# A recurrent attention kernel: two streamed weights put into PSUM by VectorE as 32-bit words, copied back by two engines, and queries turned ahead of the first half's normalization

## The chip, the core and the metric

The kernel runs on one core of a Trainium2 chip. The metric is the device time of one execution in microseconds. TensorE, VectorE, ScalarE, GpSimd and SyncE each work through their own queue of instructions in order and wait for one another by semaphores; the DMA engines move data beside them. In the profile's tables PE is TensorE, PEld its weight loads, DVE VectorE, ACT ScalarE, POOL GpSimd and SP SyncE.

## The reference

The output is the sum of the input, of an attention that carries a memory from segment to segment, and of a dense layer. Both branches read the input after a layer norm without scale and shift.

```python
xn = _layernorm(x)                                  # x: 1 x 2048 x 1024, bf16
# branch A: 64 segments of 32 rows, one after the other, M = 8 memory rows
for s in range(64):
    h = concat([mem, xn[:, 32*s:32*s+32]])          # 40 rows
    q, k, v = h @ Wq, h @ Wk, h @ Wv                # 1024 -> 32 heads x 128
    p = softmax(where(mask, q @ k.T / sqrt(128), -1e9))
    o = (p @ v) @ Wo                                # 40 x 1024
    mem = o[:, :8]                                  # memory of the next segment
    outs.append(o[:, 8:])
# branch B
gelu(xn @ w1 + b1, approximate=True) @ w2 + b2      # 1024 -> 3584 -> 1024
return x + concat(outs) + B
```

The mask has a row for each query and a column for each key: memory queries see every key, the others the keys up to their own place, `(idx[:, None] < M) | (idx[:, None] >= idx[None, :])`. Each segment needs the memory that the segment before it made, so the segments can't run side by side.

## The kernel before, in words

**First part, up to about 419 us.** Layer norm and the dense branch: four groups of 512 rows, with w1 and w2 in SBUF. In its last group the places that w1, w2 and their intermediate results leave are filled with attention weights.

**Second part.** The 64 segments. The weights Wq, Wk, Wv and Wo, 32 MB together, are cut into 64 units of 512 KB (128 partitions x 2048 bf16). A segment uses every unit once, in a fixed order: eight K units of the first half of the heads ("half 0"), eight Q units of half 0, K and Q of half 1, V of both halves, then sixteen units of Wo (the O phase). 46 units stay in SBUF. 18 are "streamed": they come again in every segment through a ring of six slots (tile name `u`). When TensorE has used a streamed unit, `unit_done` calls `start_stream`, which fills the freed slot with the next streamed unit, by a DMA from a copy in DRAM (`Wc_K`, `Wc_Q`, `Wc_V`, `Wc_O`) on SyncE's queue.

Two of the 18 come from PSUM and not from DRAM: `IN_PSUM`, the Q unit 4 of half 0, and `IN_BANKS`, the O unit 14. They lie in four PSUM banks (`kept`), put there in segment 0 by `keep`. In later segments `start_stream` copies them back into a slot (L247), two copies of 128 x 1024 bf16 each: those of IN_PSUM begin when the first K unit of the segment is done, those of IN_BANKS when O unit 7 is done ("in the K phase" and "in the O phase" below). `keep` in the kernel before goes through TensorE: it transposes 128 x 128 blocks into the bank `mixed`, copies them to SBUF on VectorE and ScalarE, and transposes them back into `kept`. The second unit's two halves wait for it in `d_oL` and `half_home`.

**Main rows and left rows.** A segment multiplies its 8 memory rows and 24 of its 32 new rows as "main rows" (`hT`); the last 8 new rows of four segments ("left rows", `hL`) are multiplied together once in four segments, each weight in a segment of its own. With i4 the segment's number modulo 4: Q of half 0 in i4 = 1, Q of half 1 in i4 = 2, K of half 0 in i4 = 3, K of half 1 in i4 = 0, V of half 0 in i4 = 0, V of half 1 in i4 = 3, Wo in i4 = 1. Segment 0 does all K, Q and V. The turned left queries are kept in `qL`; where the next group's will overwrite queries that are still needed, `keep_q` first saves these in spare columns of the bank `mixed` (`qS`), and `q_left` takes them from `qL` or, at i4 = 2 and 3 for half 0 and at i4 = 3 for half 1, from `qS`.

**Inside a segment.** `half_pass` issues the products of one half of one weight into a PSUM accumulator (`acc`, three banks, handed out by `new_acc` and `let_go`) and calls the functions in `at` after the named units. `turn_k` and `turn_q` copy an accumulator to SBUF (ScalarE, L758) and transpose it in blocks of 32 (VectorE, L772); `turn_kL` and `turn_qL` do the same for left rows with VectorE alone. `scores` multiplies queries and keys into `mixed` (L816, L822), takes the exponential (ScalarE, L828) and applies the mask (VectorE, L833). `sums` adds the exponentials by matmul into `mixed` (L841, L847), takes Ln and twice Exp on ScalarE (L852, L855), and multiplies with the result on VectorE (L862, L866); `values` multiplies by V (L881, L887) and copies out (L895). The scores of half 0 are computed after the first Q unit of half 1, their sums after its last; those of half 1 after V units 0 and 4 of half 1. At the end, `put_mem` (L282, L286) puts the new memory rows into `hT`.

The order on each engine is that of the program: the schedule is written out by hand. A framework adds the semaphore waits from what instructions read and write. So where a function is called decides what stands behind what.

Of the kernel before, what the change touches and what calls it, by code (L numbers as in the profile page):

```python
# [10 lines left out]
BF16 = mybir.dt.bfloat16  # L11
# [6 lines left out]
P = 128  # L18
# [68 lines left out]
def kernel(  # L87
# [151 lines left out]

    def start_stream(slot):  # L240
        if not starts:
            return
        n = starts.popleft()
        unit, t = streams[n], slab(slot)
        if unit in kept_in:
            for c0, bank in kept_in[unit]:
                nc.vector.tensor_copy(out=t[:, c0:c0 + 1024], in_=bank)  # L247
# [45 lines left out]
    with tc.tile_pool(name="ma", bufs=2) as ma, tc.tile_pool(name="mps", bufs=6, space=PSUM) as mps:  # L293
# [191 lines left out]
        for tg in range(4):  # L485
# [81 lines left out]
            else:  # L567
# [7 lines left out]
                put_mem(o_sb, nxt["hT"], mps.tile([P, 512], F32, name="ps"))  # L575
                pss = [mps.tile([P, 512], F32, name="ps") for _ in range(6)]
# [28 lines left out]
                nc.sync.dma_start(out=d_oL[:, :], in_=Wo_v[:, h + 1, :])  # L605
# [6 lines left out]
    with tc.tile_pool(name="late", bufs=1) as late, \  # L612
# [28 lines left out]
        kept = banks.tile([P, 4, 1024], BF16, name="kept")  # L641

        def copy_bits(out, in_):

            nc.vector.tensor_single_scalar(out=out, in_=in_, scalar=0, op=ALU.bitwise_or)

        def keep(unit, c0, w, bank):

            turned = [late.tile([P, 512], BF16, name=f"VL{n}").rearrange("p (k t) -> p k t", k=4) for n in range(2)]
            for n in range(2):  # L650
                for k in range(4):
                    nc.tensor.transpose(trs[n][:, k, :], w[:, 512 * n + P * k:512 * n + P * (k + 1)], ident)
                (nc.scalar.copy if n else nc.vector.tensor_copy)(out=turned[n], in_=trs[n])
            for n in range(2):
                for k in range(4):
                    c1 = 512 * n + P * k
                    nc.tensor.transpose(kept[:, bank, c1:c1 + P], turned[n][:, k, :], ident)
            kept_in.setdefault(unit, []).append((c0, kept[:, bank, :]))
# [31 lines left out]
        for s in range(NSEG):  # L690
# [145 lines left out]
            def sums(u):  # L836
# [17 lines left out]
                for b in (1, 0):  # L854
# [3 lines left out]
                    )  # L858
                pdA = pd_main.rearrange("p (c b q) -> p c b q", c=4, b=2)
# [56 lines left out]

            psK, psKL = half_pass("K", 0, left_k[0], {})
# [3 lines left out]
            psQ, psQL = half_pass("Q", 0, left_q[0], {})  # L921
            if first:
                keep(IN_BANKS, 1024, d_oL, 2)
                keep(IN_BANKS, 0, half_home, 3)
                nc.sync.dma_start(out=part_home, in_=Wo_v[:, 4 * PART[1] + 2 * PART[2], 0:PART_COLS])
                copy_bits(mixed[:, 468:512].bitcast(U32), mask.bitcast(U32))
                for t in outs:
                    nc.vector.memset(t[:, :, 0:32], 0.0)
# [31 lines left out]
            at = {0: [lambda: scores(1)], 4: [lambda: sums(1)]}  # L960
# [132 lines left out]
```

## Time and profile before

| | |
|---|---|
| time, median of three | 1892.51 us (1891.93 to 1899.58) |
| span of the profiled execution | 1887.0 us |
| segment 0 of the attention | 419 to 467.6 us |
| one later segment, mean | 22.4 us |
| PE, busy | 1729.5 us (92%) |
| DVE, busy | 921.3 us (49%) |
| ACT, busy | 637.6 us (34%) |
| DVE copies from `kept` (L247) | 254, 163.3 us, 685 ns each |
| DMA, mean | 328 GB/s |

A segment's start is taken as the start of L286 in VectorE's timeline, which ends the segment before. Busy time of TensorE is not work at its peak, since matmuls overlap. A wait's row names who waited, for whom, the total, how many times and the longest, in us. A timeline's row has start, duration, engine, line, operation, tiles and shapes, and in brackets the idle time just before and what ended it; a row can stand for several instructions in a run.

### The profile page before, as it was taken

To read this page: it belongs to the slowest core of one execution; us is meant where nothing else is said; L and a number is where in the kernel's file an instruction comes from. 1 tells how busy PE (TensorE), PEld (TensorE's weight loads), DVE (VectorE), ACT (ScalarE), POOL (GpSimd) and SP (SyncE) were. 2 spreads that over 40 slices of the span, in tenths; PEclk is the share of its full clock that TensorE was granted. 3 is DMA by queue.
4 is the path that set the end of the run, shared out by engine and by line. 5 is a ranking of instruction groups with operands and counts; after the bars stand their busy time and mean duration, and the time that the engine had idled before them with its cause. 6 is when DMAs were issued, how large, how long until landed. Compare 5 with 4: busy or idle time off the path is not lost.

```text
span 1887.0 us, 72995 instructions
## 1 busy us (share of the span) xinstructions
PE 1729.5 (92%) x32255; PEld 940.0 (50%) x32275; DVE 921.3 (49%) x2222; ACT 637.6 (34%) x1356; POOL 277.2 (15%) x538
## 2 busy tenths in 40 slices
PE   7999999997998989999999999899999999988987
PEld 3444444444454545455555555455545454555544
DVE  6657474603454444444454445444444454444443
ACT  6334352502333333333333333333333333333332
POOL 0000000000341111111121111212121111111112
PEclk9999999998999999999999999999999999999999
DMA  9821211498999999999999999999999999999998
GB/s 337 269 52 45 55 47 50 172 351 278 401 395 377 372 377 356 378 391 395 391 392 383 387 369 390 370 386 387 385 398 386 392 398 380 387 380 369 376 379 325
DMA packets 220025, 618.39 MB, mean 328 GB/s; under 512 B 47243, under 2 KB 65595, under 8 KB 219708
## 3 DMA queue, kind: packets, MB, share of 16 engines
q1 hardware_dynamic: 199292, 593.57, 83.0%
q0 software_dynamic: 16320, 17.52, 2.8%
q8 instruction: 252, 4.13, 0.9%
q10 hardware_dynamic: 4096, 2.64, 0.5%
q14 instruction: 65, 0.53, 0.1%
HBM read 599.39 MB, written 30.34 MB: 334 GB/s over the span
## 4 chain that ended last, share of the span: by engine, by line
PE 67%; DMA 19%; DVE 7%; ACT 3%; issue 3%; POOL 0%; ACTq 0%; DVEq 0%; POOLq 0%; SPq 0%
PE acc L714 32%; PE ps L503 10%; PE acc L907 10%; DMA u<-Wc_K 9%; PE ps L552 8%; DMA u<-Wc_O 5%; DMA u<-Wc_Q 3%; PE ps L587 2%; ACT mixed L855 2%; PE acc L881 2%; DVE b_oL L772 1%; DMA outL_d<-half_home 1%; DVE pd_main L862 1%; PE mixed L816 1%; DVE u L247 1%
## 5 line engine op out<-in xcount | busy, mean ns | idle before, releaser
L714 PE MATMUL acc<-u,hr_home 128*32 128x512 bf16 x11520 | 781.5, 382 | 32.4 <-DMA u<-Wc_K 13.6
L714 PEld LDWEIGHTS <-hr_home 128*32 128x32 bf16 x12288 | 350.8, 97 | 321.5 <-issue 72.1
L714 PE MATMUL acc<-u,hrL 128*32 128x512 bf16 x2880 | 256.3, 381 | 12.4 <-issue 6.1
L503 PE MATMUL ps<-u 128*128 128x512 bf16 x896 | 194.9, 380 | 2.6 <-ACT u L387 2.6
L907 PE MATMUL acc<-u,d_oL 128*32 128x256 bf16 (+1 forms) x3552 | 177.2, 292 | 12.3 <-DMA u<-Wc_O 7.9
L247 DVE COPY u<-kept 128x1024 bf16<-128x1024 bf16 x254 | 163.3, 685 | 25.7 <-PE acc L907 9.1
L552 PE MATMUL ps<-u 128*128 128x512 bf16 x657 | 146.2, 379 | 0.8
L907 PEld LDWEIGHTS <-b_oL 128*32 128x32 bf16 (+1 forms) x3552 | 109.1, 98 | 75.0 <-issue 40.9
L503 PEld LDWEIGHTS <-u 128*128 128x128 bf16 x896 | 87.9, 98 | 108.4 <-issue 3.1
L907 PEld LDWEIGHTS <-d_oL 128*32 128x32 bf16 (+1 forms) x3552 | 104.4, 99 | 63.8 <-issue 20.7
L862 DVE TENSOR_TENSOR pd_main<-half_home,mixed 128x320 bf16<-128x320 bf16 x128 | 62.5, 488 | 150.1 <-ACT mixed L855 147.6
L907 PE MATMUL acc<-u,b_oL 128*32 128x256 bf16 (+1 forms) x1665 | 108.7, 290 | 19.3 <-DVE u L247 8.8
L714 PEld LDWEIGHTS <-hrL 128*32 128x32 bf16 x3072 | 90.4, 96 | 66.3 <-issue 24.7
L772 DVE STREAM_TRANSPOSE b_oL<-b_oL 128x512 bf16<-128x512 bf16 x128 | 90.6, 708 | 66.8 <-ACT b_oL L758 66.8
L907 PE MATMUL acc<-W_O,b_oL 128*32 128x256 bf16 (+1 forms) x1776 | 108.3, 289 | 4.9 <-issue 4.6
L758 ACT CAST kT<-acc 128x512 bf16<-128x512 f32 x64 | 37.5, 586 | 219.7 <-PE acc L714 219.7
L259 POOL DMA_DIRECT2D hr_home<-hr_d x58 | 32.7, 564 | 528.7 <-PE acc L714 528.7
L552 PEld LDWEIGHTS <-u 128*128 128x128 bf16 x672 | 65.3, 98 | 77.4 <-DVE g_u L519 0.4
L758 ACT CAST b_oL<-acc 128x512 bf16<-128x512 f32 x128 | 75.2, 588 | 80.5 <-PE acc L714 80.5
L833 DVE TENSOR_TENSOR half_home<-half_home,mixed 128x96 bf16<-128x96 bf16 (+1 forms) x256 | 37.6, 188 | 127.4 <-ACT half_home L828 127.3
L1002 ACT CAST d_oL<-acc 128x256 bf16<-128x256 f32 (+1 forms) x63 | 26.9, 427 | 214.2 <-PE acc L907 214.2
L855 ACT ACTIVATE mixed<-mixed,small_consts 128x160 f32<-128x160 f32 x256 | 94.3, 368 | 8.4
(129 smaller groups left out, 2033.3 us busy)
## 6 DMA issues: line engine op xcount, KB each, us to landing
u<-Wc_K SPq DMA_DIRECT2D x320, 512.0 KB
u<-Wc_V SPq DMA_DIRECT2D x256, 512.0 KB
u<-Wc_O SPq DMA_DIRECT2D x256, 512.0 KB
u<-Wc_Q SPq DMA_DIRECT2D x128, 512.0 KB
u<-Wc_O SPq DMA_DIRECT2D x64, 384.0 KB
u<-in_B_w_dram SPq DMA_DIRECT2D x14, 512.0 KB
u<-in_A_Wq_dram SPq DMA_DIRECT2D x14, 512.0 KB
u<-in_A_Wv_dram SPq DMA_DIRECT2D x12, 512.0 KB
```

Of the source, the lines that this page charges most:

```text
L247: nc.vector.tensor_copy(out=t[:, c0:c0 + 1024], in_=bank)
L503: nc.tensor.matmul(ps[:, :].rearrange("p (s t) -> p s t", t=SEG), lhsT=w1_sb[fb // 14 * 8 + kt][:, (fb % 14) * P:(fb % 14 + 1) * P], rhs=x ...
L552: nc.tensor.matmul(ps[:, :], lhsT=gts[fc // 4][:, fc % 4, t * P:(t + 1) * P], rhs=w2_sb[fc // 2][:, fc % 2, cs], start=(fc == 0), stop=(fc ...
L587: nc.tensor.matmul(pss[2 * t + nb][:, :], lhsT=gts[fc // 4][:, fc % 4, t * P:(t + 1) * P], rhs=w2_sb[fc // 2][:, fc % 2, nb * 512:nb * 512 ...
L714: nc.tensor.matmul(o, lhsT=lhs[:, i, :], rhs=m, start=(i == seq[0]), stop=(i == seq[-1]), tile_position=(0, 32 * j),)
L758: cp(out=out, in_=ps.rearrange("p (h e) -> p h e", e=32))
L772: nc.vector.transpose(out=home, in_=home)
L833: nc.vector.tensor_tensor(out=p, in0=p, in1=m[:, None, :].to_broadcast([P, 4, n]), op=ALU.min)
L855: nc.scalar.activation(out=mixed[:, 160 * b:160 * b + 160], in_=mixed[:, 0:160], func=ACT.Exp, scale=-1.0, bias=off[:, b:b + 1],)
L862: nc.vector.tensor_tensor(out=pdA.rearrange("p c b q -> p b c q"), in0=prA[:, None, :, :].to_broadcast([P, 2, 4, 40]), in1=dd, op=ALU.mult,)
L881: nc.tensor.matmul(oV[r][:, c, :, :], lhsT=V[q, c * P:(c + 1) * P], rhs=pdA[q, c, :, :], start=(c == 0), stop=False, skip_group_check=True ...
L907: nc.tensor.matmul(acc[r:r + n // 8, 0:n], lhsT=lhs[:, 4 * (i % 4) + 2 * u + k, :], rhs=w_t[:, c0:c0 + n], start=(unit == O_UNITS[0] and k ...
```

## The change

The parts:

1. `keep` writes `kept` by one VectorE instruction for each half unit, a bitwise or with 0 on 32-bit words (`copy_bits`), straight from SBUF. The two halves of IN_BANKS are put away before the first K pass of segment 0 (they were put away after its first Q pass), and the DMA that brings `d_oL` is issued before the last dense products.
2. `start_stream` copies the first 1024 columns back by `copy_bits` on VectorE and the others by a ScalarE copy.
3. In later segments `q_left` is called after unit 2 of the Q pass and `keep_q` after unit 3; they were called after the pass.
4. The two products on VectorE at the end of `sums` become `normalize`. For half 0 it is called after `turn_q` of half 1, so that VectorE turns the queries first; for half 1 its place is as before.

They are to take the put-away off TensorE's queue, relieve VectorE of half the copies, and let VectorE turn queries while ScalarE computes the reciprocal of the sums.

```diff
+    def copy_bits(out, in_):
+        nc.vector.tensor_single_scalar(out=out, in_=in_, scalar=0, op=ALU.bitwise_or)
...
             for c0, bank in kept_in[unit]:
-                nc.vector.tensor_copy(out=t[:, c0:c0 + 1024], in_=bank)
+                if c0:
+                    nc.scalar.copy(out=t[:, c0:c0 + 1024], in_=bank.bitcast(BF16))
+                else:
+                    copy_bits(t[:, c0:c0 + 1024].bitcast(U32), bank.bitcast(U32))
...
                 put_mem(o_sb, nxt["hT"], mps.tile([P, 512], F32, name="ps"))
+                nc.sync.dma_start(out=d_oL[:, :], in_=Wo_v[:, h + 1, :])
...
                 fetch_resident("xt2", "xt3")
-                nc.sync.dma_start(out=d_oL[:, :], in_=Wo_v[:, h + 1, :])
...
         def keep(unit, c0, w, bank):
-            turned = [late.tile([P, 512], BF16, name=f"VL{n}").rearrange("p (k t) -> p k t", k=4) for n in range(2)]
-            for n in range(2):
-                for k in range(4):
-                    nc.tensor.transpose(trs[n][:, k, :], w[:, 512 * n + P * k:512 * n + P * (k + 1)], ident)
-                (nc.scalar.copy if n else nc.vector.tensor_copy)(out=turned[n], in_=trs[n])
-            for n in range(2):
-                for k in range(4):
-                    c1 = 512 * n + P * k
-                    nc.tensor.transpose(kept[:, bank, c1:c1 + P], turned[n][:, k, :], ident)
+            copy_bits(kept[:, bank, :].bitcast(U32), w.bitcast(U32))
             kept_in.setdefault(unit, []).append((c0, kept[:, bank, :]))
...
+            def normalize(u):
+                prA, prB = st["pr", u]
                 pdA = pd_main.rearrange("p (c b q) -> p c b q", c=4, b=2)
...
+            if first:
+                keep(IN_BANKS, 1024, d_oL, 2)
+                keep(IN_BANKS, 0, half_home[:, :], 3)
+                nc.sync.dma_start(out=part_home, in_=Wo_v[:, 4 * PART[1] + 2 * PART[2], 0:PART_COLS])
+                copy_bits(mixed[:, 468:512].bitcast(U32), mask.bitcast(U32))
+                for t in outs:
+                    nc.vector.memset(t[:, :, 0:32], 0.0)
             psK, psKL = half_pass("K", 0, left_k[0], {})
...
-            psQ, psQL = half_pass("Q", 0, left_q[0], {})
+            at = {} if first else {2: [lambda: q_left(0)]}
+            if left_q[0] and not first:
+                at[3] = [lambda: keep_q(0)]
+            psQ, psQL = half_pass("Q", 0, left_q[0], at)
             if first:
-                keep(IN_BANKS, 1024, d_oL, 2)
-                keep(IN_BANKS, 0, half_home, 3)
...
                 turn_qL(psQL, 0)
-            q_left(0)
+                q_left(0)
             turn_q(psQ)
             if left_q[0] and not first:
-                keep_q(0)
                 turn_qL(psQL, 0)
...
+            if not first:
+                at[2] = [lambda: q_left(1)]
+                if left_q[1]:
+                    at[3] = [lambda: keep_q(1)]
             psQ1, psQ1L = half_pass("Q", 1, left_q[1], at)
             if first:
                 turn_qL(psQ1L, 1)
-            q_left(1)
+                q_left(1)
             turn_q(psQ1)
+            normalize(0)
             if left_q[1] and not first:
-                keep_q(1)
                 turn_qL(psQ1L, 1)
...
-            at = {0: [lambda: scores(1)], 4: [lambda: sums(1)]}
+            at = {0: [lambda: scores(1)], 4: [lambda: sums(1), lambda: normalize(1)]}
```

More of the change, by code (lines that the diff above doesn't have):

```diff
@@ L640 @@
         mask_left = masks_at[:, NX:].rearrange("p (g q) -> p g q", g=GRP)
[L641 to L645 removed]
+        kept = banks.tile([P, 4, 512], F32, name="kept")
         def keep(unit, c0, w, bank):
[L649 to L657 removed]
+            copy_bits(kept[:, bank, :].bitcast(U32), w.bitcast(U32))
             kept_in.setdefault(unit, []).append((c0, kept[:, bank, :]))
@@ L920 @@
                 turn_kL(psKL, 0)
-            psQ, psQL = half_pass("Q", 0, left_q[0], {})
+            at = {} if first else {2: [lambda: q_left(0)]}
+            if left_q[0] and not first:
+                at[3] = [lambda: keep_q(0)]
+            psQ, psQL = half_pass("Q", 0, left_q[0], at)
             if first:
-                keep(IN_BANKS, 1024, d_oL, 2)
-                keep(IN_BANKS, 0, half_home, 3)
[L925 to L928, printed above, removed]
                 turn_qL(psQL, 0)
-            q_left(0)
+                q_left(0)
             turn_q(psQ)
             if left_q[0] and not first:
-                keep_q(0)
                 turn_qL(psQL, 0)
```

## The prediction

> **What bounds the kernel now.** I read the page's slices first, then the windows, the waits, and last the timelines of the first segment and of one later segment.
>
> The windows: stretch, busy time by engine, granted clock, DMA share, GB/s.
>
> ```profile
> 420.00:470.00 50.00, 39.94 (x747) 21.92 (x740) 17.84 (x39) 10.92 (x23) 1.82 (x4) 0.90 0.81 279
> 480.00:580.00 100.00, 90.75 (x2024) 53.26 (x2020) 45.81 (x109) 32.27 (x75) 37.52 (x68) 1.00 1.02 396
> 1500.00:1600.00 100.00, 92.44 (x2142) 51.99 (x2133) 48.96 (x115) 33.21 (x78) 16.25 (x30) 1.00 1.00 387
> ```
>
> The reader is to see two regimes. From segment 1 on, the DMA engines have a share of 1.00 and TensorE some 90%: both are full, and neither has much to give. The first segment (419 to 467.6 us) is another place: TensorE at 80% of its time, DMA at 0.81 and 279 GB/s. Only there does something other than these two set the pace.
>
> What it is, on TensorE in the first segment (start, duration, instructions, idle time before):
>
> ```profile
> 427.16 0.40 PE L657 MATMUL kept<-pd_main,VL 128*128 128x128 bf16 x4 [0.46 <-ACT VL L653]
> ...
> 429.42 0.40 PE L657 MATMUL kept<-pd_main,VL 128*128 128x128 bf16 x4 [0.46 <-ACT VL L653]
> 429.75 0.40 PE L714 MATMUL acc<-u,hr_home 128*32 128x512 bf16 x4
> ...
> 432.82 0.40 PE L652 MATMUL mixed<-pd_main,d_oL 128*128 128x128 bf16 x4 [1.59 <-DMA d_oL<-in_A_Wo_dram]
> ```
>
> The transposes of `keep` and their copies hold TensorE from 425.2 to 429.75 and, with the wait for `d_oL`, from 431.2 to 438.3.
>
> The waits (who waited for what: total, times, longest), in all segments together:
>
> ```profile
> DVE pd_main L862 <- ACT mixed L855: 147.6, 111, 3.5
> ...
> PE mixed L816 <- DVE b_oL L772: 19.5, 30, 1.0
> ...
> PE acc L907 <- DMA u<-Wc_O: 16.6, 45, 0.9
> PE acc L714 <- DMA u<-Wc_K: 13.6, 26, 1.2
> ...
> PE mixed L816 <- DVE mixed L645: 9.1, 14, 0.7
> ...
> PE acc L907 <- DVE u L247: 8.8, 14, 0.7
> ```
>
> VectorE's large wait for the exponentials costs only what is queued behind it: the turned queries, for which TensorE waits 19.5 us. `keep_q` costs 9.1 us, the copies back 8.8 us. Together 37 us in 63 segments, against 30 us of waits for streamed weights.
>
> One segment of those whose number leaves 3 by 4 ("type 3"), on VectorE:
>
> ```profile
> 1060.32 0.70 DVE L939 STREAM_TRANSPOSE d_oL<-d_oL 128x512 bf16<-128x512 bf16 x1
> 1060.95 0.65 DVE L758 CAST kL<-acc 128x512 bf16<-128x512 f32 x1
> 1061.64 0.71 DVE L772 STREAM_TRANSPOSE kL<-kL 128x512 bf16<-128x512 bf16 x1
> 1062.40 0.49 DVE L862 TENSOR_TENSOR pd_main<-half_home,mixed 128x320 bf16<-128x320 bf16 x1
> 1062.81 0.28 DVE L866 TENSOR_TENSOR pd_left<-half_home,mixed 128x128 bf16<-128x128 bf16 x1
> 1063.01 0.22 DVE L794 COPY b_oL<-mixed 128x128 bf16<-128x128 bf16 x1
> 1063.14 0.70 DVE L772 STREAM_TRANSPOSE b_oL<-b_oL 128x512 bf16<-128x512 bf16 x1
> ```
>
> TensorE starts the sums of this half at 1060.90, long before VectorE reaches the query copy of L794.
>
> **What the Trainium skill says.** "VectorE: DVE Perf Modes", section "Walkthrough: the 8-slice pipeline in each mode": two packed 16-bit elements go through per cycle, a 32-bit element from PSUM one. So the word copy of 512 is no slower than the copy of 1024 halves; the trace agrees (681 ns for 128x1024 bf16 in L247, 685 for a cast of 128x512 f32). "ScalarE: Activation LUTs", section "What ACT_TABLE_LOAD costs": 186 ns and 0.833 ns an element, bf16 or not; the trace has 586 ns for 512, a little under it. "DMA: Bandwidth & Descriptors", section "Specifications": 435 GB/s is the ceiling of the fabric; the windows reach 396, so the stream has little more in it.
>
> **The change part by part.**
>
> *Start.* `keep` as four word copies, about 0.67 us each on VectorE, beside the K and Q passes; VectorE has 4.2 us of idle time there. TensorE loses the two stretches, 4.6 + 7.1 = 11.6 us. The wait of 2.3 us for the left queries' bank, at 450.4, where VectorE first waited for the exponentials, goes also; slow matmuls (granted clock 0.90, about 3 us) may go. New: `d_oL` came at about 432.8 behind the last resident weights, and the next streamed units are issued right after it, from 428.9, as before. TensorE then arrives some 2 us before its first Q unit of half 1. The cap is the stream: (390 - 279) GB/s over these 50 us is 14 us of transfer time, of which some is blocked ahead of 428.9. I take 12 us saved, ends 8 and 15.
>
> *Copies back.* The two halves of one slot, now on two engines, look parallel. In the built order of the changed kernel they are not: in the O phase VectorE's copy waits for ScalarE's of the same slot, in the K phase ScalarE's for VectorE's. A pair took 1.29 us; now 0.67 + 1.02 (586 + 512 x 0.84, the slope between the 320 and the 512 element casts, 426 and 586 ns; the page gives 1.04) + 0.06 to cross = 1.75. In the K phase 0.46 us more lies within the margin before the Q unit (0.5 us at the least, 1.3 mostly). In the O phase TensorE needs the slot 6 units x 0.216 = 1.3 us after the copies can start. Type 3: VectorE was held by two casts until 0.88 and done at 2.16; ScalarE now begins at 0.1, so VectorE is done at 1.83: 0.3 us better. Type 0: done at 1.38, now 1.83, of which some 0.2 us shows. Types 1 and 2 arrive later than that (512-wide products, waits for Wc_O): nothing.
>
> *Queries ahead of normalization.* The cast of the queries still stands behind the exponentials on ScalarE and ends 0.51 us after them; the transpose can start there instead of at 0.74. Scores begin 0.2 us sooner in types 1 and 3. But the two products of L862 and L866 (0.69 us) now come after the transpose, and values need them: first at 2.0 us after the exponentials, against 2.06 in type 1 and 2.30 in type 3. In type 2 values need a bank that the left queries' cast frees behind those products: 2.70 against 2.44, 0.26 us worse, while the 0.33 us won at the scores is spent waiting there.
>
> *`q_left` and `keep_q` inside the pass.* This adds a wait. They touch the bank `mixed`; the sums' matmuls write it; being earlier in the program, they are now waited for by the sums. Type 3: the query copy stands behind the cast and transpose of kL: L939's end 1061.02 + 0.58 + 0.75 + 0.25 = 1062.6, where the sums started at 1060.90: 1.7 us, with the whole V pass queued behind on TensorE. Type 2: keep_q ends about 0.36 us after L939's end; the sums began 0.15 us before that end on average: 0.5 us. Type 1 and 0: no such wait.
>
> *Sum for TensorE's chain in four segments:* type 3 1.7 - 0.2 - 0.3 = 1.2; type 2 0.5 + 0.26 = 0.76; type 0 0.2; type 1 -0.06: together about 2.0 us, in 15 groups 31 us. Not all shows: TensorE waits for weights 1.1 us in type 2 and 0.6 in type 1, and where it arrives later it waits less. On the other hand the stream is fed by the slots TensorE frees. By the gaps of unexplained origin in this trace (0 to 2.7 us a segment, 43 in all), a microsecond lost on TensorE lengthened its own segment by 0.9, and that and the next together by 0.65, with wide scatter. I take 0.4, about 12 us, with ends 0 and 0.9 (28 us).
>
> **Rivals.** *Given back (forecast):* 1892.5 - 12 + 12 = 1892. *The saturated stream absorbs the new waits:* the shares of 1.00 speak for it, the waits for DMA of only half a microsecond a segment against; 1892.5 - 12 + 2 = 1882, faster. *The new waits are paid in full and more than eat the start:* the gaps' effect speaks for it, the waits for weights against; 1892.5 - 12 + 28 = 1908, slower. *Nothing of the wait on `mixed` is real and 37 us of waits fall by half:* 1892.5 - 12 - 18 = 1862; the order of the built program speaks against it.
>
> **How the numbers follow.** Forecast 0.48, absorbed 0.25, paid in full 0.24, the last 0.03. The bound of 0.5% is 9.5 us. Faster 0.28, same 0.46, slower 0.26; a part of the forecast's case lies outside the bound on no preferred side. The range is from 1879 (start at 14, nothing lost) to 1908.
>
> **What would show it.** After: no matmuls into `kept`; segment 0 ends at about 454 instead of 467.6 (right start); the sums waiting for the query copy 1.7 us in type 3 and for `keep_q` 0.5 us in type 2 (a row of about 30 us in all); the wait of scores for turned queries down by a fifth to a third; copies back of 1.0 us on ScalarE, end to end with VectorE's. Wrong if segments of types 2 and 3 are no longer than before, if segment 0 still ends after 460, or if ScalarE's copies delay the casts behind them so that K or Q passes wait.

## The result, and the profile after

The changed kernel took 1905.76 us (median of four runs, 1903.54 to 1906.91) against 1892.22 us (four runs, 1891.34 to 1899.58) of the kernel before: a ratio of 1.0062, 95% interval 1.0035 to 1.0089. It is slower by some 12 us, clear of the noise. That is near the end of the predicted range (1908) and not at the predicted 1892.

The windows of the changed kernel, with the columns of those shown of before (stretch, busy time by engine, granted clock, DMA share, GB/s):

```profile
420.00:470.00 50.00, 41.52 (x867) 22.93 (x869) 24.30 (x51) 15.54 (x31) 6.93 (x13) 1.00 0.94 345
480.00:580.00 100.00, 91.33 (x2100) 50.75 (x2100) 41.11 (x101) 40.57 (x81) 37.28 (x68) 1.00 1.02 393
1500.00:1600.00 100.00, 87.61 (x2058) 49.52 (x2052) 41.37 (x103) 41.56 (x87) 17.10 (x33) 1.00 0.99 372
```

The first stretch is better: 345 GB/s instead of 279 (over segment 0 alone 350 instead of 268). The last is worse: TensorE's busy time falls from 92.4 to 87.6 us in 100, and the stream from 387 to 372 GB/s, while the DMA share still reads 0.99. By VectorE's timeline segment 0 now takes 36.9 us (423.4 to 460.3) instead of 48.6, and the 62 after it, up to the last new memory, 1415.8 us instead of 1392.0. So the change won 11.7 us once and lost 23.7 us over the rest. (A part of this is the clock. From 366 to 424 us the granted clock was 1.00 before and 0.94 after, and the dense part ended 4.4 us later; from 420 to 470 us it was 0.90 before and 1.00 after, so that not all of the 11.7 us is the change's doing.)

Where the 23.7 us are, in the waits of the changed kernel (who for what: total, times, longest):

```profile
PE mixed L811 <- DVE pd_left L863: 46.3, 47, 1.1
...
PE mixed L836 <- DVE b_oL L789: 19.6, 15, 1.4
PE acc L709 <- DMA u<-Wc_K: 17.4, 30, 2.0
...
PE acc L904 <- DMA u<-Wc_O: 11.1, 32, 0.9
...
PE mixed L836 <- DVE mixed L242: 6.9, 10, 1.2
```

Three rows are new, and they take the place of the 19.5 + 9.1 us that the scores waited for turned queries and `keep_q` before. L836 are the sums, L789 the query copy in `q_left` and L242 here `keep_q`: the two waits that the prediction named, 26.5 us where it had about 30. L811 are the scores, L863 the second product of `normalize`, 47 times: three segments of four. The prediction has no such wait. The waits for Wc_O fell from 16.6 to 11.1 us, but those for Wc_K rose from 13.6 to 17.4.

The same type 3 segment as before, on VectorE, in the changed kernel:

```profile
1061.74 0.70 DVE L939 STREAM_TRANSPOSE d_oL<-d_oL 128x512 bf16<-128x512 bf16 x1
1062.37 0.65 DVE L753 CAST kL<-acc 128x512 bf16<-128x512 f32 x1
1063.05 0.71 DVE L767 STREAM_TRANSPOSE kL<-kL 128x512 bf16<-128x512 bf16 x1
1063.69 0.19 DVE L789 COPY b_oL<-mixed 128x128 bf16<-128x128 bf16 x1
1065.95 0.71 DVE L767 STREAM_TRANSPOSE b_oL<-b_oL 128x512 bf16<-128x512 bf16 x1 [2.08 <-ACT b_oL L753]
1066.59 0.45 DVE L859 TENSOR_TENSOR pd_main<-half_home,mixed 128x320 bf16<-128x320 bf16 x1
1066.96 0.27 DVE L863 TENSOR_TENSOR pd_left<-half_home,mixed 128x128 bf16<-128x128 bf16 x1
```

and on TensorE:

```profile
1063.93 0.25 PE L836 MATMUL mixed<-half_home,small_consts 128*32 128x160 bf16 x4 [1.34 <-DVE b_oL L789]
...
1067.29 0.20 PE L811 MATMUL mixed<-b_oL,d_oL 128*32 128x40 bf16 x4 [0.92 <-DVE pd_left L863]
```

The sums start when L789 has read `mixed` (1063.88). The queries are turned at 1066.66, but the scores of half 1 start at 1067.29, just after L863 has ended at 1067.23. The scores read neither result of `normalize`. They write columns 0 to 223 of `mixed`, and `normalize` reads its reciprocals from columns 0 to 319: the write has to wait for the read. (The sums share no column with `q_left`, which reads from 340 on. They wait for it all the same, so that the framework's wait needs only the tile in common. The tile `mixed` is one whole bank, so that these runs can't tell tile from bank.)

Means by type, worked out from these two traces (us; segments 2 to 61; "to" is from the start of the scores of half 0, or from the end of the last exponential of `sums`):

| | type 1 before, after | type 2 | type 3 | type 0 |
|---|---|---|---|---|
| scores to sums, half 0 | 1.81, 1.81 | 2.46, 3.04 | 1.85, 3.47 | 2.00, 1.85 |
| exponentials to scores of half 1 | 1.50, 1.89 | 1.61, 1.88 | 1.52, 1.88 | |
| exponentials to first values | 2.11, 2.48 | 2.50, 2.61 | 2.38, 2.65 | |
| whole segment | 23.77, 23.27 | 21.15, 21.53 | 22.83, 24.29 | 22.18, 22.41 |

The chain is longer by 1.62 (type 3) and 0.58 (type 2) at the sums, and by 0.37 + 0.11 + 0.27 at the values. That is 3.0 us in four segments, and the segments grew by 1.6. (Some expectations below have 3.4 us: they add 0.4 for the O phase of type 0, 5.90 us long after and 5.41 before. But with the start alone, whose copies back are those of before, it takes 5.85, so that the change didn't make this.)

### The profile page after: what moved, and what is told of

Its sections match the earlier page's. It is cut to its first block, busy times and chain, and to the rows that moved or that the text cites. A ratio compares the mean times of both kernels' runs of the same rounds, so it can differ in the third digit from the quotient of the medians.

```text
span 1905.2 us, 73166 instructions
## 1 busy us (share of the span) xinstructions
PE 1721.2 (90%) x32211; PEld 925.8 (49%) x32211; DVE 843.4 (44%) x2095; ACT 760.0 (40%) x1479; POOL 276.1 (14%) x538
## 4 chain that ended last, share of the span: by engine, by line
PE 62%; DMA 20%; DVE 7%; ACT 6%; issue 4%; POOL 0%; ACTq 0%; DVEq 0%; POOLq 0%; SPq 0%
PE acc L709 27%; DMA u<-Wc_K 13%; PE ps L510 10%; PE acc L904 9%; PE ps L559 8%; DMA outL_d<-half_home 4%; DMA u<-Wc_O 2%; PE ps L595 2%; ACT mixed L850 2%; PE acc L878 2%; DVE d_oL L939 1%; ACT b_oL L753 1%; DVE pd_main L859 1%; DMA u<-Wc_V 1%; PE mixed L811 1%
## 5 line engine op out<-in xcount | busy, mean ns | idle before, releaser
L709 PE MATMUL acc<-u,hr_home 128*32 128x512 bf16 x11520 | 775.9, 380 | 32.1 <-DMA u<-Wc_K 17.4
L709 PEld LDWEIGHTS <-hr_home 128*32 128x32 bf16 x12288 | 345.8, 96 | 318.2 <-issue 60.0
L252 ACT COPY u<-kept 128x1024 bf16<-128x1024 bf16 x127 | 128.5, 1012 | 174.7 <-DVE u L242 102.8
L904 PE MATMUL acc<-u,d_oL 128*32 128x256 bf16 (+1 forms) x3552 | 172.9, 291 | 7.0 <-issue 3.4
L767 DVE STREAM_TRANSPOSE b_oL<-b_oL 128x512 bf16<-128x512 bf16 x128 | 91.1, 711 | 166.1 <-ACT b_oL L753 166.0
L242 DVE TENSOR_SCALAR u<-kept 128x512 uint32<-128x512 uint32 x127 | 87.5, 689 | 76.3 <-ACT u L252 55.8
L847 ACT ACTIVATE mixed<-mixed 128x160 f32<-128x160 f32 x128 | 36.9, 288 | 169.8 <-PE mixed L842 168.2
L518 ACT ACTIVATE g_xb<-ps,b1col 128x512 bf16<-128x512 f32 x112 | 76.8, 686 | 61.5 <-PE ps L510 60.4
L859 DVE TENSOR_TENSOR pd_main<-half_home,mixed 128x320 bf16<-128x320 bf16 x128 | 59.9, 468 | 93.2 <-ACT mixed L850 90.2
L767 DVE STREAM_TRANSPOSE kT<-kT 128x512 bf16<-128x512 bf16 x64 | 45.5, 711 | 118.0 <-ACT kT L753 118.0
```

The costliest lines, as they stand in the source:

```text
L252: nc.scalar.copy(out=t[:, c0:c0 + 1024], in_=bank.bitcast(BF16))
L518: nc.scalar.activation(out=xb[:, :], in_=ps[:, :], func=ACT.Identity, bias=b1col[:, fb:fb + 1], scale=1.0)
L709: nc.tensor.matmul(o, lhsT=lhs[:, i, :], rhs=m, start=(i == seq[0]), stop=(i == seq[-1]), tile_position=(0, 32 * j),)
L767: nc.vector.transpose(out=home, in_=home)
L859: nc.vector.tensor_tensor(out=pdA.rearrange("p c b q -> p b c q"), in0=prA[:, None, :, :].to_broadcast([P, 2, 4, 40]), in1=dd, op=ALU.mult,)
L904: nc.tensor.matmul(acc[r:r + n // 8, 0:n], lhsT=lhs[:, 4 * (i % 4) + 2 * u + k, :], rhs=w_t[:, c0:c0 + n], start=(unit == O_UNITS[0] and k ...
```

## The experiments

Every ratio is against the kernel before, run beside it on the same chip. A reading "of 18 us" is a difference of two ratios times 1893 us. The intervals of single ratios are 0.2 to 0.3% to either side, so that such a difference is good to some 6 us, and to 7 or 8 where few runs were made. Means by type and sums of waits come from one trace of each kernel.

### One part at a time

**`q_left(1)` and `keep_q(1)` after the pass**, the rest as changed:

```diff
-            if not first:
-                at[2] = [lambda: q_left(1)]
-                if left_q[1]:
-                    at[3] = [lambda: keep_q(1)]
             psQ1, psQ1L = half_pass("Q", 1, left_q[1], at)
             if first:
                 turn_qL(psQ1L, 1)
-                q_left(1)
+            q_left(1)
+            if left_q[1] and not first:
+                keep_q(1)
             turn_q(psQ1)
```

> The changed kernel with q_left and keep_q of half 1 called after the pass again (ahead of turn_q). Theory: the sums' matmuls write the bank mixed and so wait for the query copy behind the cast and transpose of kL (1.6 us in type 3) and for keep_q (0.6 us in type 2). Without that 2.2 us of TensorE's chain go in four segments, 33 us in 15 groups, of which about half shows: 1906 - 16 = 1890 us, and the rows of sums waiting for L789 and for keep_q are gone. Rival (these calls cost nothing, the loss is in the copies back and in the late normalization): 1905 us.

Measured: 1888.22 us, ratio 0.9965 (0.9943 to 0.9987). The sums of type 3 begin 1.89 us after the scores again, and type 3 segments take 22.87 us as before the change. The two calls inside the pass cost 18 us.

**Normalization ahead of the queries again**, the rest as changed:

```diff
-                7: [lambda: sums(0)],
+                7: [lambda: sums(0), lambda: normalize(0)],
...
             turn_q(psQ1)
-            normalize(0)
```

> The changed kernel with the normalization of half 0 put back right after the exponentials, ahead of the turned queries. Theory: the scores of half 1 write the bank that the normalization reads, so turning the queries first only puts the products between the transpose and the scores (from the end of the exponentials to the scores 1.9 us, against 1.5 before). Undone: 0.4 us less in types 1, 2 and 3, 1.2 us in four segments, about half of it shown: 1906 - 9 = 1897 us. Rival (queries ahead help, as meant): 1908 us or more. Third (no one waits long enough for it to matter): 1906.

Measured: 1896.64 us, ratio 1.0002 (0.9981 to 1.0023), 11 us better than the changed kernel. The scores start 1.39 us after the exponentials instead of 1.88. Turning the queries first was meant to bring the scores forward, and it put them back.

**Both copies back on VectorE**, the rest as changed:

```diff
-                if c0:
-                    nc.scalar.copy(out=t[:, c0:c0 + 1024], in_=bank.bitcast(BF16))
-                else:
-                    copy_bits(t[:, c0:c0 + 1024].bitcast(U32), bank.bitcast(U32))
+                nc.vector.tensor_copy(out=t[:, c0:c0 + 1024], in_=bank.bitcast(BF16))
```

> The changed kernel with both copies from PSUM back on VectorE as copies of 1024 bf16. Theory: the two copies on two engines run one after the other, 1.75 us a pair against 1.29: O phase of type 0 0.4 us and of type 2 0.2 us longer, of type 3 0.2 us shorter. Undone, 0.4 us less in four segments, half of it shown: 1903 us. Rival A (the serial copies are the main loss, also by delaying ScalarE's casts in the K phase): 1890 us or less. Rival B (relieving VectorE helps): 1909 us or more.

Measured: 1910.75 us, ratio 1.0067 (1.0036 to 1.0097): no different from the changed kernel. ScalarE's copy takes 1.01 us, and the two of a slot do run one after the other, here in an O phase of the changed kernel:

```profile
1050.11 1.01 ACT L252 COPY u<-kept 128x1024 bf16<-128x1024 bf16 x1
1051.16 0.69 DVE L242 TENSOR_SCALAR u<-kept 128x512 uint32<-128x512 uint32 x1 [1.09 <-ACT u L252]
```

But that costs nothing that these runs can tell.

**The start alone**: the kernel before with part 1.

> The kernel before with the first part of the change alone: kept written by VectorE's word copies, the fetch of d_oL and the put-away moved forward; all later segments as before. Theory: segment 0 takes 37 us in place of 48.6, of which slow matmuls of a lower clock explain up to 3; later segments unchanged: 1892 - 10 = 1882 us. Rival (the saturated stream takes it back in the segments after): 1890 us with segments 1 to 4 longer than before.

Measured: 1883.77 us, ratio 0.9931 (0.9908 to 0.9953): the start is worth 13 us (9 to 17), and the segments after it are as before (mean 22.5 us).

The parts add up: -13 (start) + 18 (left queries in the pass) + 11 (normalization last) + 0 (copies) = +16 us, against +12 measured, which agrees within the errors. The two calls of half 0 that also moved into a pass stayed there in all runs but the start alone; what they cost was not measured apart.

### Which of the two delays at the sums counts

**`q_left(1)` after the pass in type 3 alone:**

```diff
             if not first:
-                at[2] = [lambda: q_left(1)]
+                if i4 != 3:
+                    at[2] = [lambda: q_left(1)]
...
-            if first:
+            if first or i4 == 3:
                 q_left(1)
```

> The changed kernel, with q_left(1) called after the Q pass of the second half in the segments whose number leaves 3 by 4 alone; in those of type 2, q_left(1) and keep_q(1) stay inside the pass. Theory: the wait of the sums costs what it is long where it stands, and about half of it reaches the end: of type 3's 1.6 us in each of 15 segments (24 us) some 12 come back, so about 1894 to 1896; type 3's sums begin 1.9 us after the scores of the first half instead of 3.5, type 2's stay at 3.0. Rival: type 2's 0.6 us matter as much (VectorE's order there, not the length of the wait): then half or less of the 18 us that both together brought comes back, 1898 or more.

Measured: 1890.57 us, ratio 0.9971 (0.9950 to 0.9992), as with all calls after the pass, though type 2's sums still come 2.88 us after its scores. So type 3's 24 us (1.6 in 15 segments) cost 17, and type 2's 9 us about 1, each within some 6 us. The 17 us lie above the 12 expected, but a flat half for both, 12 and 4.5, isn't excluded.

Type 2 has waits for Wc_O that could take its delay up (0.93 us a segment before, 0.48 after; type 3 has none). The traces speak against it: they are 0.59 us here, with the sums late, and 0.60 with all calls after the pass, where the sums come at 2.31. What shrinks instead is the matter of the last part of the experiments.

### Is it the bank?

**Reciprocals to SBUF**, on top of the calls after the pass: the second exponentials are written into `pd_main`, so that normalization reads nothing of `mixed`.

```diff
-                        out=mixed[:, 160 * b:160 * b + 160], in_=mixed[:, 0:160], func=ACT.Exp, scale=-1.0,
+                        out=pd_main[:, 160 * b:160 * b + 160], in_=mixed[:, 0:160], func=ACT.Exp, scale=-1.0,
...
-                dd = mixed[:, 0:320].rearrange("p (b c q) -> p b c q", b=2, q=40)
+                dd = pd_main[:, :].rearrange("p (b c q) -> p b c q", b=2, q=40)
```

The tile is bf16, so that the reciprocals are rounded to bf16, `pd_main` takes the columns' order of the reciprocals, and the product that overwrites it (L859 in the changed kernel) comes second.

> The kernel in which q_left(1) and keep_q(1) come after the pass, and in which the second exponentials also go to SBUF, as bf16, into the tile that the normalized probabilities take, so that normalization reads nothing of the bank mixed. The reciprocals are so rounded to bf16 before the product. Theory: the scores of the second half wait for normalization only because their matmuls write the bank that it reads; here they begin when the queries are turned, about 1.3 to 1.4 us after the exponentials instead of 1.88, in three segments of four, 1.5 us less in four segments; half of it reaches the end, 11 us in 15 groups: a ratio of about 0.991 against the kernel before, where q_left after the pass alone gave 0.9965. Rival: the scores are late for what stands ahead of normalization on VectorE and the place of normalization does not matter: they stay at 1.88 and the time stays at 0.9965. Other rival: they begin sooner but the values, which need the products, take the whole gain back: 0.9965 as well, with the scores at 1.4.

Measured: 1884.28 us, ratio 0.9933 (0.9910 to 0.9956). The scores begin 1.27 to 1.29 us after the exponentials in the three types, and the row of 46.3 us is gone. TensorE's waits in this kernel, by rows:

```profile
PE acc L904 <- issue: 18.7, 24, 2.3
PE acc L904 <- DMA u<-Wc_O: 18.2, 46, 1.6
PE mixed L811 <- DVE b_oL L767: 14.9, 45, 0.4
```

What the scores still wait for is the turned queries (L767), as intended. The cause of the missed wait is shown. Against the run with the calls after the pass, the reciprocals lie elsewhere (with the changes that this brings, named above), the two products of `normalize` change places, and the order on every engine is otherwise the same. `normalize` still comes right after `turn_q`, and the scores no longer wait for it. Of 1.8 us that the scores gained in four segments, 0.9 reached the values (1.97, 2.50 and 2.42 us after the exponentials instead of 2.46, 2.62 and 2.70), 13 us in all, and about 6, no more than the error, the end.

**`q_left(1)` right after the scores of half 0, `keep_q(1)` in the K pass of half 1:**

```diff
-            psK1, psK1L = half_pass("K", 1, left_k[1], {})
+            at = {1: [lambda: keep_q(1)]} if left_q[1] and not first else {}
+            psK1, psK1L = half_pass("K", 1, left_k[1], at)
...
-                0: [lambda: scores(0), lambda: nc.vector.transpose(out=nat_home, in_=nat_home)],
+                0: [lambda: scores(0)] + ([] if first else [lambda: q_left(1)])
+                + [lambda: nc.vector.transpose(out=nat_home, in_=nat_home)],
...
-            if not first:
-                at[2] = [lambda: q_left(1)]
-                if left_q[1]:
-                    at[3] = [lambda: keep_q(1)]
```

> The kernel in which q_left(1) stands right after the scores of the first half, ahead of VectorE's transpose of the keys, and keep_q(1) in the K pass of the second half. Theory: the copies out of mixed are then done before the sums want to write that bank, so that the sums wait for nothing new, and the cast and copy no longer stand between the pass and the turned queries: sums 1.9 us after the scores in type 3 at the most, 2.3 in type 2, as with both calls after the pass, and a little off the queries' way: a ratio of 0.994 to 0.9965. Rival: q_left ahead of the transpose delays the transpose of the keys by 0.2 us, and all of VectorE's chain with it: no better than 0.9965 or worse by 3 us.

Measured: 1888.73 us, ratio 0.9963 (0.9945 to 0.9982). That is the time of the calls after the pass (0.9965): an early copy in the right place costs nothing and brings nothing that these runs can tell.

**Both together**, the reciprocals in SBUF and the calls in those two places:

> Both: q_left(1) right after the scores of the first half, keep_q(1) in the K pass of the second half, and the second exponentials in SBUF as bf16 (the reciprocals rounded to bf16 before the product), so that normalization reads nothing of mixed. Theory: the gains lie on the same chain at different places and add, with half of each showing: about 0.989 to 0.991 against the kernel before, which would be the fastest of all. Rival: the saturated stream takes what is left, and the time is that of the start alone, 0.993, or more.

Measured: 1884.48 us, ratio 0.9924 (0.9895 to 0.9953). This, the reciprocals in SBUF alone (0.9933) and the start alone (0.9931) can't be told apart; all three beat both kernels. Here TensorE waits 24.7 us for Wc_O where the changed kernel waited 11.1: a part of the gain turns into other waits.

### Where the other half goes

TensorE's chain grew by 3.0 us in four segments and the segments by 1.6. Did waits for the stream take up the rest? To see it, transfers were taken away. **One streamed unit of Wo less** in each segment from 2 on (its products read a resident unit), in four kernels:

```diff
-    streams = [unit for _ in range(NSEG) for unit in ORDER if IS_STREAMED[unit]]
+    LESS = STREAMED_O[1]
+    streams = [unit for k in range(NSEG) for unit in ORDER if IS_STREAMED[unit] and (k < 2 or unit != LESS)]
...
+            if unit == LESS and s >= 2:
+                return res_tiles[RESIDENT[-1]]
             if IS_STREAMED[unit]:
```

Before:

> The kernel before with a lighter stream: from segment 2 on, the second of the six streamed units of the output projection is not transferred, and its products read a resident unit instead (that part of the output is computed from the wrong weights). It takes 0.5 MB of 17 units' worth from each of 62 segments, 33 MB, about 82 us of transfer at 395 GB/s. Theory: TensorE's chain sets the pace and the stream only takes part of what happens on it, so that of the 82 us only TensorE's waits for streamed weights, 31 us, and little more come off: 1850 to 1865, a ratio of 0.975 to 0.984. Rival: the stream sets the pace, and most of the 82 us come off: 1815 to 1830, 0.957 to 0.965.

Changed:

> The changed kernel with the same lighter stream (the second streamed unit of the output projection left out of the transfers from segment 2 on, its products made from a resident unit). Theory: part of the new delays was absorbed in waits for weights, which are now gone, so more of them shows: of 3.4 us in four segments (51 us) nearly all, less 13 for the start: 20 to 35 us above the kernel before with the lighter stream, where with the full stream it was 12. Rival: the share of about a half has another cause than the stream, and the distance stays at about 12 us.

Calls after the pass:

> The kernel with q_left(1) and keep_q(1) after the pass, with the same lighter stream. Theory: with the stream out of the way the delay of the sums shows in full, 1.6 us in type 3 and 0.7 in type 2: 28 to 35 us faster than the changed kernel with the lighter stream, where with the full stream it was 18. Rival: type 2's delay costs nothing for another reason than its waits for weights, and the distance stays 18 to 22 us.

Normalization first:

> The kernel with normalization ahead of the queries again, with the same lighter stream. Theory: the values then begin 0.75 us sooner in four segments, 11 us, and nearly all of it shows: 10 to 14 us faster than the changed kernel with the lighter stream, as with the full one, 11. Rival: what counts is the scores, which begin 1.5 us sooner in four segments: 20 us or more.

Measured: 0.9911 (0.9877 to 0.9944), 0.9977 (0.9960 to 0.9994), 0.9904 (0.9872 to 0.9935) and 0.9929 (0.9903 to 0.9955). Within the errors the distances are those of the full stream: changed to before 12 us, calls after the pass 14, normalization first 9. My theory fell: 82 us less of transfer took only 17 us off the kernel before, and no more of the delays showed. The DMA engines stayed nearly as busy, with less moved (the kernel before with the lighter stream, by its windows):

```profile
480.00:580.00 100.00, 90.82 (x2040) 50.39 (x2034) 45.70 (x111) 32.91 (x77) 37.89 (x69) 0.97 0.99 371
1500.00:1600.00 100.00, 90.98 (x2133) 51.16 (x2129) 48.62 (x114) 32.96 (x77) 16.19 (x30) 1.00 0.97 358
```

TensorE's waits for weights did go, from 31 us to 3. Two rows of TensorE's waits tell what came instead. The kernel before, O phase and K, Q, V passes (L907, L714; "issue" is waiting for nothing that the profile shows):

```profile
PE acc L714 <- issue: 18.1, 28, 1.9
...
PE acc L907 <- issue: 9.7, 14, 1.7
```

The same with the lighter stream (L910, L717):

```profile
PE acc L910 <- issue: 27.3, 29, 2.7
PE acc L717 <- issue: 21.8, 27, 2.6
```

One of them, in the middle of the products of one resident unit:

```profile
912.52 0.27 PE L910 MATMUL acc<-W_O,b_oL 128*32 128x256 bf16 x1
...
915.50 0.40 PE L910 MATMUL acc<-W_O,b_oL 128*32 128x256 bf16 x7 [2.71 <-issue]
```

Seven of the eight products of this group begin 2.71 us after the first has ended, with operands that were there all along. Such gaps stand in a pattern. Counted in TensorE's instructions (products, weight loads and the few waits for semaphores), the distance from one such gap to the next is a multiple of 256, within 3, for each of the 52 gaps over 0.3 us in the segments of the kernel before and of the 66 with the lighter stream. From one gap that another engine or a transfer ended to the next, it is so for none of 112 and one of 73. The table of queues of the kernel before has the rest:

```profile
q8 instruction: 252, 4.13, 0.9%
```

252 packets of 16 KB: TensorE's 64,649 instructions are 252 blocks of 256 and a half. In the trace of the DMA packets each of these gaps ends 1.4 us (1.26 to 1.51 for eight in ten) after a packet of this queue has landed; the one above landed at 914.23. Of the 112 gaps that another engine or a transfer ended, 8 end within the same range after a packet (1.20 to 1.64 us). So TensorE's gaps of unknown origin (64 of them, 42 us, in the kernel before) are waits for its next block of instructions.

The Trainium skill, "Runtime: NRT & Kernel Launch", section "Instruction fetch mechanics", says that an engine's instructions are refilled in blocks of 16 KiB (256 instructions), the next one fetched over a DMA queue while the current one runs, and that crossing a block is mostly hidden. The trace agrees on blocks and queue, and not on "hidden": with the DMA engines full, 64 of some 230 blocks in the segments came late in the kernel before, 79 with the lighter stream.

**Six units less of sixteen**, to see whether the full DMA engines make the blocks late (list of units in `LESS`, else as above). Before:

> The kernel before with a much lighter stream: six of the sixteen units that come from DRAM in a segment are not transferred from segment 2 on, and their products read a resident unit (the output is made from the wrong weights there). TensorE's gaps with no cause in the records each end 1.4 us after a 16 KB packet of the instruction queue has landed, and 256 instructions apart. Theory A: these blocks of instructions come late because the DMA engines are full; with a share of some 0.7 they come in time, the gaps fall from 42 to 68 us to under 15, and nearly all of TensorE's waits for weights (31 us) and half or more of these gaps come off: 1830 to 1850, a ratio of 0.965 to 0.976. Theory B: the blocks take that long whatever else is moved: the gaps stay at 50 to 70 us and the time at 0.988 to 0.993, as with one unit less.

Changed:

> The changed kernel with the same much lighter stream (six units of sixteen left out, their products from a resident unit). Theory A: nothing absorbs the new waits any longer; they are 3.4 us in four segments, 51 us, less the start: 25 to 38 us above the kernel before with the much lighter stream. Theory B: the late blocks of instructions go on absorbing, and the distance stays at about 12 us.

Calls after the pass:

> The kernel with q_left(1) and keep_q(1) after the pass, with the same much lighter stream. Theory A: the delay of the sums shows in full, in type 2 too: 28 to 35 us faster than the changed kernel with the much lighter stream. Theory B: 14 to 20 us, as before.

Measured: 1780.40 us, 0.9412 (0.9391 to 0.9433); 1902.55, 1.0047 (1.0026 to 1.0068); 1876.83, 0.9925 (0.9898 to 0.9953). The kernel before, by its windows:

```profile
480.00:580.00 100.00, 94.23 (x2160) 52.68 (x2155) 48.53 (x119) 33.83 (x79) 40.45 (x74) 1.00 0.85 291
1500.00:1600.00 100.00, 96.01 (x2313) 58.06 (x2308) 51.06 (x121) 35.23 (x83) 17.36 (x32) 1.00 0.82 265
```

At a share of 0.82 to 0.85 the gaps fell to 12 us (68 with one unit less), and the waits for weights to nothing: theory A holds on the blocks. The gain is larger than it forecast: segments 2 to 61 became 106 us shorter, and the gaps of 0.15 us and more account for 64 of them. Of the other 42 us, 20 to 30 are the beginnings of the same waits. The profile counts a wait from the modelled end of the product before; counted from that product's start, the 214 waits of the kernel before hold 183 us and the 105 of this one 89. The rest is not settled.

The two changed kernels gained little, for a reason of their own, in the waits of the changed one:

```profile
ACT u L253 <- DVE u L243: 200.0, 63, 4.4
...
PE mixed L290 <- ACT d_oL L1009: 80.7, 62, 2.0
```

With other units in the slots, ScalarE's copy back, and its wait for VectorE's half, came to stand ahead of the cast (L1009) from which TensorE makes the new memory rows. TensorE waited for it in 62 segments. (The calls after the pass are 23 us faster than the changed kernel here, between the two theories.) Part 2 is harmless only as long as the slots come free when they do with the full stream.

**The same with both copies on VectorE**, changed, and changed with the calls after the pass:

> The changed kernel with both copies back on VectorE, and the much lighter stream (six streamed units of sixteen left out from segment 2 on). In the changed kernel with the lighter stream, ScalarE's copy of 1.0 us came to stand ahead of the cast that TensorE's last products of a segment read, and TensorE waited 1.3 us for it in every segment; here ScalarE has no copy. Theory: nothing absorbs the new waits any longer, so that the distance to the kernel before with the same stream (1780) is 3.4 us in four segments, 51 us, less 13 for the start, 38 us: 1810 to 1825, and 75 us and more under the changed kernel with the lighter stream. Rival: the copies on ScalarE had no part in that, and it stays at about 1900.

> The same with q_left(1) and keep_q(1) after the pass. Theory: the delay of the sums, 1.6 us in type 3, shows in full when nothing absorbs it: 24 to 33 us under the changed kernel with VectorE's copies and this stream, so about 1785 to 1797. Rival: 14 to 18 us, as with the full stream.

Measured: 1803.71 us, 0.9533 (0.9491 to 0.9576), and 1779.54 us, 0.9397 (0.9358 to 0.9435). The first is 99 us faster than with ScalarE's copies: they were the reason. The 24 us of type 3's sums now cost 24 to 26: in full, within the error. Against the kernel before with the same stream, the changed one is 23 us behind and not 38. Two terms of the 38 are not there: `keep_q` hardly holds up the sums of type 2 (2.25 us after the scores, 2.17 in the kernel before with this stream; why it is done in time here was not looked into), and type 0's O phase is no longer (4.44 us, 4.59 before).

What TensorE waited for in segments 2 to 61, from the traces (idle times of 0.15 us and more, us):

| kernel | other engines | weights | instruction blocks | length |
|---|---|---|---|---|
| before | 41 | 31 | 42 | 1348.9 |
| changed | 83 | 29 | 32 | 1372.6 |
| calls after the pass | 57 | 22 | 47 | 1357.8 |
| reciprocals in SBUF | 35 | 27 | 64 | 1353.8 |
| before, one unit less | 48 | 3 | 68 | 1344.6 |
| before, six less | 38 | 0 | 12 | 1242.6 |
| changed, copies on VectorE, six less | 73 | 0 | 8 | 1274.7 |
| the same, calls after the pass | 51 | 0 | 10 | 1251.7 |

With the full stream, what one column loses another gains: taking 26 us of the changed kernel's waits on other engines away (second to third row) gave 15 us of late blocks back. One pair shows little, since late blocks come by chance: the start alone, with the segments of before, has 54 us of them where before has 42. All ten traces with the full stream show it. Their waits on other engines go from 31 us (both together) to 87 (both copies on VectorE). A straight line through the ten has 0.50 us less of waits for weights and blocks, and 0.46 us more of length, for each us more of waits on other engines (correlations -0.85 and 0.91). That is the missing half. A reading that fits is that transfers and blocks have longer to arrive when TensorE comes late for another reason; it isn't shown apart. With six units less there is hardly anything to take the delays up (last two rows: 22 us of waits, 23 us of length).

## Why the prediction was wrong, point by point

- **Start**, -12 us: right on what goes, and the start alone gave 13 us. It ended at 460.3 and not at 454, just past the sign of being wrong (460), because the dense part before it ended 4.4 us later in that profile. Of the 11.7 us by which segment 0 is shorter, some 4 are the better clock: in traces where segment 0 lost the same 3.4 us to it, it takes 47.1 us with the old start (two) and 39.1 and 39.4 with the new.
- **Copies back**: right on what the program does (one after the other, ScalarE's 1.01 us for 1.02). On the size the runs show only that it is about nothing, 1 us within some 8.
- **"Scores begin 0.2 us sooner in types 1 and 3"**: the step that failed. They begin 0.27 to 0.39 us later, in three types. I looked for who reads what `normalize` writes, and found the values. I didn't ask who writes what it reads. The scores write `mixed`, as I had used in the next paragraph for `q_left`. In the kernel before this wait was there and cost nothing, since normalization stood ahead of the turned queries in VectorE's queue. The values are therefore at 2.48 and 2.65 us in types 1 and 3 where the step had 2.0. Undoing it gave 11 us, where the step's own account had a loss of 0.26 us in type 2 alone (under 2 us in all, at the share).
- **`q_left` and `keep_q` in the pass**: right in mechanism and in length: 1.6 us for 1.7 in type 3, 0.6 for 0.5 in type 2. Of the offsets in type 3, the 0.2 us at the scores became the delay above, and of the 0.3 us at the copies the waits for them show 0.1 (0.59 us a segment before, 0.49 after).
- **"I take 0.4"**: near, since about half of the delays reached the end, but in part by luck. I had the waits for weights take up the rest. In the line through the ten traces they take 0.16 us of each us, and the late blocks 0.34. These I had seen as gaps of unknown origin, and I didn't expect them to shrink. Whether one share holds for all types is open (17 of type 3's 24 us, 1 of type 2's 9, each within some 6 us; my sum had 7 and 4.6).
- **Sum**: 2.0 us in four segments and +12 us forecast; 3.0 us and +24 in the trace. The missed wait, 11 us by its run, is most of the difference of 12; the share, a half for 0.4, goes the same way.
- **Rivals**: "paid in full" (1908) was nearest in time, but not for its reason: the waits weren't paid in full, there were more of them.
- **What bounds**: "both are full" was the wrong reading of a DMA share of 1.00. With 6% less to move the share stayed at 0.97 to 0.99 in the two windows shown, and the time fell by 0.9%. The share didn't tell what set the pace.

## What to carry to other kernels

When an instruction moves back in an engine's queue, list who writes what it reads as well as who reads what it writes; a shared tile, here a PSUM bank, makes waits that the old order hid. Price a delay by how much of it other waits take up, measured over several kernels: here they took up about half of it beside the full stream, and next to nothing with six units less. A wait removed beside a full DMA comes back in part as another: compare the sum over all of TensorE's waits, "issue" among them, and not the row that went.

## What the runs showed of the hardware that was not expected

- TensorE's instructions arrive in blocks of 256 (16 KB) over the DMA engines. At a DMA share of 0.96 to 1.02 TensorE lost 32 to 68 us of some 1350 waiting for late blocks, up to 2.7 us at once; at 0.79 to 0.85, 8 to 12 us (the kernels of the table).
- The granted clock of TensorE went down in single stretches at 0.50, of 3.4 or 6.8 us (but for the last of a trace). One of 6.8 us near the end of the dense part, at 368 to 369 us, is in 9 of the 19 traces: segment 0 began at 422.8 to 423.4 us in these, and at 418.8 to 419.6 in the other ten. Two profiles can so differ by 4 us there, whatever the change.
- Two engines that each write one half of a tile wrote one after the other, in either order (1055.24 us VectorE, 1055.96 ScalarE; 1050.11 ScalarE, 1051.16 VectorE). These are the waits that the framework sets; whether the engines could write side by side, no run shows.
